# Linear attention and a gated feed-forward layer on one core: rows, maxima and exps as separate pieces, first v on ScalarE's queue, half a projection cast by Pool's DMA, a new order

## The chip, the core and the metric

The kernel runs on one core of a Trainium2 chip. Its engines work from queues of their own: TensorE (PE; PEld is its weight load), VectorE (DVE), ScalarE (ACT), GpSimd (POOL) and SyncE (SP, which here only issues DMAs). The metric is the device time of one execution in microseconds; less is better.

## The reference, cut to what matters

```python
def _attn_ref(q, k, v, w_phi):            # q, k, v: 8 batches, 8 heads, 576 rows, 64 columns
    def phi(x):
        proj = np.einsum('bhsd,df->bhsf', x, w_phi)                   # 64 -> 128
        proj = proj - np.max(np.abs(proj), axis=-1, keepdims=True)
        return np.concatenate([np.exp(proj), np.exp(-proj)], axis=-1) # 256 features
    q_p, k_p = (phi(q), phi(k))
    kv = np.einsum('bhsf,bhsd->bhfd', k_p, v)
    z = np.sum(k_p, axis=2)
    num = np.einsum('bhsf,bhfd->bhsd', q_p, kv)
    den = np.einsum('bhsf,bhf->bhs', q_p, z)[..., None] + 1e-06
    return num / den

def _moe_ref(x, w_gate, w_val, w_out):    # x: 4608 rows of 512 (the heads side by side)
    gate = np.maximum(x @ w_gate, 0.0)    # 512 -> 1536
    val = x @ w_val
    return gate * val @ w_out             # 1536 -> 512
```

The kernel returns `_moe_ref` of the attention's output, in fp32.

## The kernel before, in words

**Tiles.** Of each batch's 576 rows, 512 are handled as four chunks of 128 (`C = 4`), and the last 64, the tail, are put together with another batch's. A key item is one pair of heads of one batch, four per batch (`NU = 4`). For it TensorE transposes the keys (L235; DVE copies the result to `tT`, L238), multiplies 64-row halves with `w2` (bf16, `w_phi` twice one below the other) into two PSUM banks (rows, L260); DVE takes the maximum of the absolute value of each row (`mk`, L242); ACT takes exp of the rows with both signs (`kp`, L280) and of the maxima with both signs (`ek`, L284); POOL multiplies v with `ek` (`vs`, L246, and a column of `ek` itself, L252); TensorE multiplies `kp` with `vs` to kv and z (L309), adds the tail's share (L317; for that POOL makes `ekm`, L294, and `vsm`, L246), and DVE (batch 0) or ACT copies the 128x260 result (`kv`, L325). From batch 2 on, keys and queries are transposed by DMA.

A query piece projects columns (L343) and rows (L260), ACT takes exps (`qp`, L354 and L356), DVE maxima (`mq`), ACT a scale from them (`cq`, L362). Numerators and denominators (L379) are combined on DVE (L388, L391, reciprocal L394) and scaled on POOL (`xu`, L396), and `xu` is transposed to `xT` (L406 on TensorE for batches 0 and 1, by DMA later). The feed-forward layer takes `xT` with the value and gate weights (L434), for batch 0 in steps of 16 matmuls of 128 columns, later of four of 512; ACT copies the value half to `val_sb` (L443), DVE makes `h` from both (L447); `h` times `w_out` (L460) is copied and stored.

**The order.** `Plan.add` collects pieces of work: a function that issues a few instructions, with the engine times that a planner assumed, what a piece needs and gives, and the PSUM banks it takes. `ORDER` is a list, found by a search beforehand, of piece numbers with their banks: `43:76` issues piece 43 with banks 7 and 6, and `z22:0` issues fillers, 22 units of 128 columns of zeros times zeros into bank 0 (L930), which compute nothing that is used. All instructions of all engines are issued in this one order, and each engine runs its own in that order. So an instruction that waits holds all later ones on its engine. The fillers of `ORDER` come to 176 units, all ahead of piece 397, the first feed-forward step.

**Loads.** Before the planned part, SP's queue gets the first pairs of batch 0 in fp32, `k0 k1 v0 k2 v1 k3`, the tail of the keys (`kt`), `v2 v3` and the tail of v (`vt`). ACT's queue gets `w_phi` twice (`wf`, L939), and ACT casts each half into `w2` (L963). POOL makes the identities (L956), then copies one element of the second key pair (`gate`, L958), so that POOL and the loads behind it wait for that pair. Loads that cast fp32 to bf16 go through POOL's queue and stand in POOL's instruction stream: queries and keys (`qn`, `kn`), the three thirds each of the value, gate and output weights (`wv_sb`, `wg_sb`, L210; `wo_sb`, L217), the tails of later batches (L176) and mixed queries (L167). `LOADS` names them as pieces 0 to 42, and `ORDER` places them:

```python
LOADS = """q0 wv0 wg0 kt1 k1 wv1 wg1 vt1 v1 wv2 wg2 q1 wo0 wo1 wo2 qm0 k2 kt2 vt2 v2 q2 k3 v3 q3 qm1
...
```

In the built program the DMAs of POOL's queue take eight semaphores in turn, and those of SP's and ACT's queues eight others; a DMA that takes a semaphore is issued once the DMA that had it before has landed.

**The key item as one piece.** In `k_group` rows, maxima, exps and `ek` were one piece (`krows`), in three forms: maxima and exps of the two halves crosswise (`wide=False`, the first two items), exps first (`"late"`, the third), and maximum first (`wide=True`). `q_group` did the same for queries.

Of the kernel before, what the change touches and what calls it, by code (L numbers as in the profile page):

```python
# [19 lines left out]
class Plan:  # L20
# [8 lines left out]
    def add(  # L29
        self, rank, kind, fn, ops, needs=(), gives=None, take=(), drop=(), after=(), banks=(), hold=None, free=None  # L30
    ):
        self.pieces.append(
            (rank, kind, fn, ops, needs, gives, take, drop, after, banks, hold, free)
        )
# [12 lines left out]
ORDER = """0 z22:0 43:76 47:5 44:6 z4:4 51:0 48:1 55:3 z4:4 59:0 52:6 z26:5 60:4 3 4 1 7 5 45 8 56:2 9 49 61  # L47
z38:1 62:0 z4:1 81:1 72:6 z18:7 82:4 z5:7 63:06 84:2 67 50:3 57 46:4 53 88:5 85:6 2 68:24 11 58:0
54:1 6 83 89:4 64:01 65:6 z27:7 69:71 10 96:2 18 90 92:3 z25:0 66:6 73:40 70:7 16 z3:2 397:6 381:3
74:04 389:2 97:6 13 382:3 71:4 93:0 17 86 91:5 130 75:23 391:4 76:6 94 133 98 399:7 390:3 100:2  # L50
109:6 78:50 383:1 101:36 398:2 392:5 95:0 79:1 132 102:63 15 400:2 99:5 87:0 77:1 80:3 384:4 12 14
118 103:76 104:5 106:01 395:2 393:6 385:7 107:2 126 386:3 110:46 403:0 396:1 401:2 145 19 111:63
146:0 387:5 394:2 402:3 20 137 105:4 119 127:6 408:2 21 115:34 112:01 128 409 411:5 410 120:36 138:0
147 131 412 413 113:2 116:6 167 139 141 388:7 24 22 405:3 108:4 406 142:0 143 134:6 404:2 177 414:4
135 149 117:5 407 23 415 114:5 140:2 121:01 419:5 122:67 416 123:5 26 150:20 417:7 129 423:4 169
418:6 435:5 151:02 178:6 424:4 136:5 436:2 148:3 433:0 124:1 425:4 173 144:2 181 170:6 158 182:0 203
426:5 420:4 168 434:3 437:2 152:56 179 153:7 431:4 29 429:3 430:6 154 183 438:7 155:01 194 217 427:2
159:35 432:7 125 421:2 28 25 156:1 439:0 160:63 171 174:1 422:5 185 184:0 428:3 440:4 175 164:76
444:5 157 161:34 162:1 441:2 27 180:0 442 176:0 165:1 172:6 445 166 163 186:30 447:7 443 446 187:03
211 215 212:5 448 33 450:2 216 451 188:34 189:0 449 230 452 35 191:16 469:7 213 453:0 195:24 226  # L60
192:1 30 454:6 214 473:7 461:0 196:41 231:6 474:3 470:0 462:1 463:2 190 200:54 457:3 32 201:0 467:1
222 193 227:6 223:2 464:4 302 468:5 218 252 253 234 31 458:0 232 455:1 465:4 262 204 197:76 228
475:5 198:0 466:2 229:3 243 235:60 456:4 459:5 205:20 199 460:4 471:7 254 224 288 202 236:50 219:2
472:4 477:7 476:0 220 206:15 233:6 478 36 263:4 270 480:0 225:6 34 481 221:3 479 207:21 483:4 237:35
238:1 240:67 264 482 505:2 486:5 258 259:0 255:2 484 487 260 300 489:7 241:6 488 485 497:6 490:0
208:1 507:2 266 256 289 209:3 506:7 244:04 508:6 499:7 495:2 239 245:03 38 267:5 496:7 500:2 493:3
242 498:4 246:70 503:1 247:2 261:4 249:03 301 307 257:1 250:7 504:6 501:5 290:31 509:0 319 494:7
491:5 271:13 315 268 308:6 492:0 502:5 510:3 511:4 512:2 248 269:5 251 279 265:3 272:06 39 316:4
513:2 296 519:3 520 516:6 40 273:70 521 303 37 276:14 328 514 274:5 515 275 297:3 304:0 529:7 311
277:5 522:2 517 278 518 539:5 523 41 525:3 524 280:06 526:4 305 317 545:5 337 540:3 309 281:60 312:4  # L70
527:2 530:3 338 298 546:0 285:16 210 339 313 533:7 547:3 286:0 282:64 283:5 318:1 364 291:27 534:0
343 310:1 351 531:6 284 528:1 532:7 535:0 320:53 344:1 306:7 347 548:0 537:3 541:4 538:0 536:5 42
287 543:6 542:7 292:43 544:2 314:1 293:0 552:3 561:1 573:2 553 321:06 352:4 549:2 345 550 294:6
555:7 322:01 554 551 355 323:1 565:6 325:05 556 558:6 559 560 557 329:42 562:6 299 295 577:7 566:0
330:13 348:5 373 583:7 574:0 567:3 326:4 578:1 331:20 575:4 584:1 568:0 332:7 576:6 563:5 324 334:74
333 564:3 569:2 349 581:1 356:64 340:2 571:0 579:1 582:4 591:5 335:6 570:7 336 346:4 594:6 357:20
572:7 341 585:4 580:0 592 588:7 353 589 354:3 374 350:2 342:1 327 586 593 361:03 601:2 587 358:15
595 359:0 603:2 362:3 590 611:4 597:5 596 365:02 598:7 602:4 612:5 366:62 607:4 608:5 360 599:0
370:12 619:3 600:0 371:2 620:7 363 613:1 615:0 375:24 604:1 609:0 614:7 367:65 617:4 368:7 618:3
376:52 624:4 605:1 369 610:0 606:7 616:6 621:5 627:7 372 622 623 625 630:6 626 631 377:53 628 655:4  # L80
645:0 378:5 639:1 632 629 633:0 634:1 646:2 640:0 637:1 651:7 652:0 647:6 379:7 638:5 656:4 643:3
641:2 642:1 648:0 649:7 635:6 636:5 644:7 650:6 657:0 663:7 380 666:1 653:2 667 677:3 654:2 658
669:6 659 668 660:2 664 661 671:3 662 665 681:6 670:5 682:7 672:6 689:0 673:7 678:1 679:0 674:2
675:1 676:0 680:7 685:6 691:5 687:7 686:6 692:0 690:7 688:1 683:0 684:2 693:1 696:0 694 695 702:7
703:6 704:5 699:7 697 700 698 701"""
# [6 lines left out]
def kernel(  # L92
# [172 lines left out]
    def k_group(st, n=4, at=0, wide=True):  # L265

        banks = rows_group([(par, st["T"]) for par in range(2)], n)
        if "kp" not in st:
            st["kp"] = st["pool"].tile([P, 2, 2, 4, F], BF16, name="kp")
        kp = st["kp"][:, :, :, at : at + n]  # L270
        ek = st["ek"] = sb_s.tile([P, 8, 2], FP32, name="ek", bufs=8)[:, 0 : 2 * n]
        mk = sb_s.tile([P, 8], FP32, name="mk")[:, 0 : 2 * n]
        m = mk.rearrange("p (j i) -> p i j", i=2)
        for par in range(1 if wide else 2):
            mine = slice(0, 2) if wide else slice(par, par + 1)
            other = slice(0, 2) if wide else slice(1 - par, 2 - par)
            if wide != "late":
                row_max(m[:, mine], banks[:, mine])
            for s, sign in ((0, 1.0), (1, -1.0)):
                nc.scalar.activation(kp[:, s, other], banks[:, other], AF.Exp, scale=sign)  # L280
            if wide == "late":
                row_max(m, banks)
        for s, sign in ((0, -1.0), (1, 1.0)):
            nc.scalar.activation(ek[:, :, s], mk, AF.Exp, scale=sign)  # L284
# [47 lines left out]
    def q_group(st, i, places):  # L332
# [13 lines left out]
        banks = rows_group(halves)  # L346
# [5 lines left out]
        for s, sign in ((0, 1.0), (1, -1.0)):  # L352
            if x is y:
                nc.scalar.activation(x["qp"][:, s], cols, AF.Exp, scale=sign)  # L354
            else:
                nc.scalar.activation(x["qp"][:, s, a], cols[:, 0], AF.Exp, scale=sign)  # L356
                nc.scalar.activation(y["qp"][:, s, b], cols[:, 1], AF.Exp, scale=sign)  # L357
        m = st["m"][:, 2 * lo : 2 * lo + 8]
# [66 lines left out]
    def ffn_pieces(g):  # L425
# [102 lines left out]
        for t in range(3 if g == B else 4):  # L528
            for part in range(3):
                ops = [("PE", NF * (0.0025 + DM / 2400))]  # L530
                if part == 2:
# [16 lines left out]
                    banks=[(1, None)] if part == 0 else [],  # L548
                    hold=(g, "po", t) if part == 0 else None,
                    free=((g, "po", t), 1) if part == 2 else None,  # L550
# [22 lines left out]
    def load(fn, us, gives, take=(), eng="POOL", issue=0.9):  # L573
        plan.add(
            "load", None, fn, [(eng, issue), ("DMA", us, 0, 2.6)], gives=gives, take=take
        )
# [6 lines left out]
    def k_pieces(rank, st, start, ops, needs, take, name, banks, late=(), n=4, at=0, wide=True):  # L583
        plan.add(rank, "kT", start, ops, needs, (rank, "T"), take, late, banks=banks)
        us = 0.1 + n * 0.287, 0.08 + n * 0.206
        if wide == "late":
            ops = [("PE64", 0.055 * n), ("ACT", us[1]), ("ACT", us[1], 0), ("DVE", us[0]), ("ACT", 0.21)]
            last = 3
        elif wide:
            ops = [("PE64", 0.055 * n), ("DVE", us[0]), ("ACT", us[1]), ("ACT", us[1], 1)]  # L590
            ops += [("ACT", 0.21, 1)]
            last = 3
        else:
            ops = [
                ("PE64", 0.23),
                ("DVE", 0.6, 0),
                ("ACT", 0.48, 0),
                ("ACT", 0.48, 0),
                ("DVE", 0.6, 3),
                ("ACT", 0.48, 1),  # L600
                ("ACT", 0.48, 1),
                ("ACT", 0.21, 4),
            ]
            last = 6
# [3 lines left out]
            lambda: k_group(st, n, at, wide),  # L608
            ops,
            [(rank, "T")],  # L610
            (rank, "rows", 0),
            [],
            [(tag, 0, n, key) for tag, n, key in name],
            banks=[(2, last)],
        )

    def k_item(rank, b, u):
# [4 lines left out]
        def start():  # L622
# [3 lines left out]
            kn = inputs["kn", b]  # L626
# [10 lines left out]
        else:  # L637
# [4 lines left out]
            else:  # L642
# [9 lines left out]
                [("T4", 1, rank)],  # L652
                banks,
                [("kn" if b else "vn1", 0, NU, ("k", b))],
                wide=b > 0 or (False, False, "late", True)[u],
            )
        plan.add(
            rank,
# [414 lines left out]
```

## Time and profile before

| | us |
|---|---|
| median of 5 runs | 391.26 (388.54 to 393.53) |
| the profiled execution | 391.61 |
| its span, first to last instruction | 389.8 |
| TensorE busy | 378.0 |
| ScalarE, VectorE, GpSimd busy | 239.6, 238.6, 155.2 |
| fillers (L930), 48 matmuls | 14.0 |
| feed-forward matmuls with value and gate weights (L434) | 95.3 and 94.5 |
| matmuls with w_out (L460) | 100.0 |

A line of the timeline has the start, the duration, the engine (with q: its DMA issues), the line of the code, the operation, the tile written and those read, shapes and how many of them in a row; in brackets, the idle time before and what ended it. A line of the busy times by stretches has the stretch, its length, the busy time of PE, PEld, DVE, ACT and POOL (with the number of instructions), the granted TensorE clock (1.00 is full), the busy share of the DMA engines (it can pass 1, as transfers overlap) and GB/s. A line of the DMA issues has the tiles, the queue, the number of issues, KB of each and the median time from issue to landing. In the slices, each of 40 digits stands for a fortieth of the span, 9.7 us, in tenths.

### The profile page before, as it was taken

How to read it: one execution, taken by the hardware profiler on the slowest of the kernel's cores; microseconds unless marked ns; L12 is line 12 of the kernel's file. 1: busy time of each engine (PE TensorE's matmuls, PEld its weight loads, DVE VectorE, ACT ScalarE, POOL GpSimd, SP SyncE). 2: the span in 40 equal slices, each digit the busy share in tenths (PEclk: the TensorE clock that was granted, in tenths of full speed). 3: DMA queues.
4: the chain of work that ended last, by engine and by line, in shares of the span. 5: the costliest groups of instructions: out<-in, count | busy, mean ns of one | idle time of the engine just before them, and what ended most of it. 6: DMA issues, size and time to landing. Idle time of an engine off the chain costs nothing.

```text
span 389.8 us, 8990 instructions
## 1 busy us (share of the span) xinstructions
PE 378.0 (97%) x3620; PEld 210.0 (54%) x3620; DVE 238.6 (61%) x413; ACT 239.6 (61%) x480; POOL 155.2 (40%) x176
## 2 busy tenths in 40 slices
PE   8599999999999999999999999999999999999995
PEld 4266998555564455645454645445554444444452
DVE  4568988777885788658864866487347622522230
ACT  5639868788768889578768774576455414323411
POOL 5785963795562873381506731413420100100000
PEclk9979999999999999999999999999999999999999
DMA  8999999999399999647649930230122021002003
GB/s 219 205 238 198 170 109 211 180 240 142 49 231 171 157 162 224 104 124 123 167 77 200 193 42 3 82 69 15 27 82 56 13 69 54 14 3 108 0 5 105
DMA packets 92506, 45.22 MB, mean 116 GB/s; under 512 B 58288, under 2 KB 87984, under 8 KB 92464
## 3 DMA queue, kind: packets, MB, share of 16 engines
q1 hardware_dynamic: 63984, 30.55, 35.6%
q0 software_dynamic: 27840, 13.50, 28.2%
q10 hardware_dynamic: 640, 0.59, 0.5%
q8 instruction: 28, 0.46, 0.5%
q14 instruction: 14, 0.11, 0.1%
HBM read 37.81 MB, written 9.44 MB: 121 GB/s over the span
## 4 chain that ended last, share of the span: by engine, by line
PE 92%; DMA 4%; ACT 1%; SPq 1%; DVE 1%; issue 0%; ACTq 0%
PE pall L434 49%; PE pall L460 23%; PE pall L379 5%; PE pall L260 4%; PE pall L309 4%; PE pall L343 3%; DMA kt<-in_k_dram 2%; DMA vn<-in_k_dram 1%; PE pall L930 1%; PE pall L235 1%; PE pall L317 1%; PE pall L487 1%; SPq L158 1%; ACT kp L280 0%; ACT qp L354 0%
## 5 line engine op out<-in xcount | busy, mean ns | idle before, releaser
L447 DVE SCALAR_TENSOR_TENSOR h<-pall,val_sb 128x512 bf16<-128x512 f32 x108 | 72.7, 685 | 53.1 <-PE pall L434 43.3
L443 ACT CAST val_sb<-pall 128x512 bf16<-128x512 f32 x108 | 62.4, 597 | 66.8 <-PE pall L434 63.4
L460 PE MATMUL pall<-wo_sb,h 128*128 128x512 bf16 x420 | 100.0, 379 | 0.0
L434 PE MATMUL pall<-xT,wv_sb 128*128 128x512 bf16 (+1 forms) x528 | 95.3, 321 | 0.0
L434 PE MATMUL pall<-xT,wg_sb 128*128 128x512 bf16 (+1 forms) x528 | 94.5, 321 | 0.0
L396 POOL TENSOR_TENSOR xu<-u,r 128x512 bf16<-128x512 f32 x36 | 37.4, 1042 | 142.2 <-DVE r L394 88.4
L280 ACT ACTIVATE kp<-pall 128x1024 bf16<-128x1024 f32 (+1 forms) x78 | 70.3, 958 | 23.6 <-DVE mk L242 22.5
L246 POOL TENSOR_TENSOR vs<-vn,ek 128x1024 bf16<-128x1024 f32 x32 | 61.1, 1908 | 21.5 <-ACT ek L284 19.6
L434 PEld LDWEIGHTS <-wv_sb 128*128 128x128 bf16 x576 | 46.5, 98 | 39.8
L434 PEld LDWEIGHTS <-wg_sb 128*128 128x128 bf16 x576 | 46.1, 98 | 39.7
L242 DVE TENSOR_REDUCE mq<-pall 128x8 f32<-128x1024 f32 x36 | 44.0, 1221 | 34.8 <-PE pall L260 15.9
L460 PEld LDWEIGHTS <-h 128*128 128x128 bf16 x420 | 38.5, 98 | 41.0
L388 DVE TENSOR_TENSOR t<-pall,cq 128x455 f32<-128x455 f32 (+3 forms) x80 | 33.5, 419 | 25.0 <-PE pall L379 24.6
L242 DVE TENSOR_REDUCE mk<-pall 128x8 f32<-128x1024 f32 (+1 forms) x39 | 43.7, 1135 | 6.7 <-PE pall L260 3.4
L356 ACT ACTIVATE qp<-pall 128x512 bf16<-128x512 f32 x60 | 36.5, 608 | 6.3 <-PE pall L343 6.3
L470 ACT COPY out_sb<-pall 128x512 f32<-128x512 f32 x35 | 20.5, 590 | 31.9 <-PE pall L460 31.0
L391 DVE TENSOR_TENSOR u<-pall,t 128x455 f32<-128x455 f32 (+3 forms) x80 | 34.2, 428 | 6.9 <-POOL xu L396 0.5
L357 ACT ACTIVATE qp<-pall 128x512 bf16<-128x512 f32 x60 | 36.8, 613 | 0.0
L379 PEld LDWEIGHTS <-qp 128*128 128x128 bf16 x640 | 28.1, 98 | 13.4 <-ACT qp L354 0.5
L379 PE MATMUL pall<-kv,qp 128*128 128x65 bf16 x640 | 30.6, 193 | 0.4 <-DVE kv L325 0.3
L309 PEld LDWEIGHTS <-kp 128*128 128x128 bf16 x512 | 18.9, 97 | 3.6
L309 PE MATMUL pall<-vs,kp 128*128 128x65 bf16 x512 | 20.5, 193 | 0.0
(67 smaller groups left out, 273.3 us busy)
## 6 DMA issues: line engine op xcount, KB each, us to landing
out_dram<-out_sb SPq DMA_DIRECT2D x32, 256.0 KB, 2.5
vn<-in_v_dram SPq DMA_DIRECT2D x7, 1024.0 KB, 8.2
qn<-in_q_dram POOLq DMA_DIRECT2D x8, 512.0 KB, 8.8
kn<-in_k_dram POOLq DMA_DIRECT2D x7, 512.0 KB, 8.1
wv_sb<-in_moe_w_val_dram POOLq DMA_DIRECT2D x3, 512.0 KB, 19.6
wg_sb<-in_moe_w_gate_dram POOLq DMA_DIRECT2D x3, 512.0 KB, 11.3
wo_sb<-in_moe_w_out_dram POOLq DMA_DIRECT2D x3, 512.0 KB, 9.5
vn<-in_k_dram SPq DMA_DIRECT2D x4, 256.0 KB, 3.6
```

Of the source, the lines that this page charges most:

```text
L242: nc.vector.tensor_reduce(m, banks, axis=AX.X, op=ALU.max, apply_absolute_value=True)
L246: nc.gpsimd.tensor_tensor(dst[:, :, :, 0:D], src[:, :, None, :].to_broadcast([P, *dst.shape[1:3], D]), ek[:, :, :, None].to_broadcast([P, ...
L280: nc.scalar.activation(kp[:, s, other], banks[:, other], AF.Exp, scale=sign)
L309: nc.tensor.matmul(kv_ps[:, hh, s, :], lhsT=st["kp"][:, s, c % 2, 2 * hh + c // 2], rhs=st["vs"][:, 4 * hh + c, s, :], start=(hh == s == c ...
L356: nc.scalar.activation(x["qp"][:, s, a], cols[:, 0], AF.Exp, scale=sign)
L357: nc.scalar.activation(y["qp"][:, s, b], cols[:, 1], AF.Exp, scale=sign)
L379: nc.tensor.matmul(banks[s][:, i], lhsT=x["qp"][:, s, slot, P * blk : P * (blk + 1)], rhs=kvs[b, h // 2][:, h % 2, s, :],)
L396: nc.gpsimd.tensor_tensor(x["xu"], x["u"][:, :, 0:D], r.to_broadcast([P, 8, D]), op=ALU.mult)
L434: nc.tensor.matmul(ps[:, n * i : n * (i + 1)], lhsT=w[:, dc, P * fi : P * fi + P], rhs=xT[:, dc, lo:hi], start=(dc == 0), stop=(dc == NDC ...
L443: nc.scalar.copy(st["val", step], ps)
L447: nc.vector.scalar_tensor_tensor(st["h2"][:, fis[0] : fis[-1] + 1, lo:hi], ps.rearrange("p (a b) -> p a b", b=n), 0.0, st["val", step].rea ...
L460: nc.tensor.matmul(st["po", t], lhsT=st["h2"][:, fi, P * t : P * t + P], rhs=wo_sb[:, fi, :], start=(fi == 0), stop=(fi == NFC - 1),)
```

## The change

1. **Smaller pieces.** `k_group` becomes `k_rows`, `k_max` with `k_scales`, and `k_exps`, which `ORDER` places one by one; the crosswise form stays one piece behind its rows, for the first two items alone. `q_group` becomes `q_rows`, `q_exps` and `q_max`. There are 849 pieces in place of 705.
2. **First loads.** `w_phi` goes once to `wf` on ACT's queue, and its second half goes straight to `w2` by a casting DMA of POOL's queue (in the built program, POOL's first DMA). The four pairs of batch 0's v go on ACT's queue. Of batch 0's keys the first two pairs stay on SP's queue in fp32, and the last two go by POOL's queue in bf16, into the unused room of the same tile. The `gate` copy is gone. Key and v tails follow on SP's queue.
3. **The order** is searched anew, with other assumed times for a few loads. Its fillers come to 143 units. `LOADS` is as before.

```diff
-    def k_group(st, n=4, at=0, wide=True):
...
+    def k_rows(st, n=4):
+        st["rows"] = rows_group([(par, st["T"]) for par in range(2)], n)
+
+    def k_exps(st, n, at, pars=slice(0, 2)):
...
+        for s, sign in ((0, 1.0), (1, -1.0)):
+            nc.scalar.activation(kp[:, s, pars], st["rows"][:, pars], AF.Exp, scale=sign)
+
+    def k_max(st, n, pars=slice(0, 2)):
...
+    def k_crosswise(st):
+
+        for par in range(2):
+            k_max(st, 4, slice(par, par + 1))
+            k_exps(st, 4, 0, slice(1 - par, 2 - par))
+        k_scales(st, 4)
...
+    def wide_pieces(rank, st, n, at, done=lambda: None):
+        plan.add(
+            rank,
+            "kmax",
+            lambda: (k_max(st, n), k_scales(st, n)),
...
+        plan.add(
+            rank,
+            "kexp",
+            lambda: (k_exps(st, n, at), done()),
...
-    for hh in range(2):
-        nc.scalar.dma_start(out=wf[D * hh : D * (hh + 1)], in_=w_phi)
+    nc.scalar.dma_start(out=wf[0:D], in_=w_phi)
+    nc.gpsimd.dma_start(out=w2[D:P], in_=w_phi)
...
-    for step in "k0 k1 v0 k2 v1 k3 t v2 v3".split():
-        if step == "t":
-            load_first_tail(0)
-        else:
-            heads = slice(2 * int(step[1]), 2 * int(step[1]) + 2)
-            load_kqv(0, step[0] + "n", k if step[0] == "k" else v, nc.sync, FP32, heads)
+    late_k = inputs["kn", 0][:, 4:6].bitcast(BF16).rearrange("p a c d -> p (a c d)")
+    late_k = late_k.rearrange("p (h c d) -> p h c d", h=4, c=C)
+    for u in range(NU):
+        if u < 2:
+            load_kqv(0, "kn", k, nc.sync, FP32, slice(2 * u, 2 * u + 2))
+        load_v(0, 2 * u, 2 * u + 2, nc.scalar)
+    load_first_tail(0)
     load_tail(inputs["vt", 0], 0, 1, v, nc.sync)
...
-    gate = singles.tile([P, 1], FP32)
-    nc.gpsimd.tensor_copy(gate, inputs["kn", 0][:, 2, 0, 0:1])
+    for u in range(2):
+        nc.gpsimd.dma_start(
+            out=late_k[:, 2 * u : 2 * u + 2],
+            in_=k[0, 4 + 2 * u : 6 + 2 * u, 0:SF, :].rearrange("h (p c) d -> p h c d", c=C),
+        )
...
-        nc.scalar.copy(w2[rows], wf[rows])
+    nc.scalar.copy(w2[0:D], wf[0:D])
...
-ORDER = """0 z22:0 43:76 47:5 44:6 z4:4 51:0 48:1 55:3 z4:4 59:0 52:6 z26:5 60:4 3 4 1 7 5 45 8 56:2 9 49 61
+ORDER = """z22:0 43:76 48:5 44:6 45 z6:4 49:0 z14:2 53:5 0 50 z12:4 54:2 65:7 3 59:6 4 56 1 5 z9:4 66:4 46 67
...
```

In the built order of POOL's queue the DMAs run: half of `w_phi`, the last two key pairs of batch 0, q of batch 0, k of batch 1, value thirds 1 and 2, q of batch 1, value third 3, gate third 1, four parts of the keys' tail of batches 2 and 3, gate third 2, two parts of a mixed q, gate third 3, k of batch 2, the thirds of `w_out`. Before they ran: q of batch 0, k of batch 1, value thirds 1 to 3, gate third 1, q of batch 1, gate thirds 2 and 3, k of batch 2, `w_out` third 1, four parts of the tail. TensorE's lines move from L235, L260, L309, L343, L379, L406, L434 and L930 to L240, L265, L323, L357, L402, L429, L457 and L999.

## The prediction, made before the result was known

> **What bounds the kernel now.** I read the page's first lines, then the busy time by stretches. It splits the span into a start-up, a dense part and a tail.
>
> ```profile
> span 389.8 us, 8990 instructions
> ...
> PEclk9979999999999999999999999999999999999999
> DMA  8999999999399999647649930230122021002003
> ```
> ```profile
> 36.14:385.05 348.91, 348.78 (x3328) 192.81 (x3325) 216.60 (x372) 217.31 (x433) 132.33 (x144) 1.00 0.60 106
> 0.00:36.14 36.14, 29.26 (x294) 17.18 (x295) 22.01 (x42) 21.66 (x47) 22.87 (x33) 0.91 1.15 216
> 385.05:389.80 4.75, 0.00 (x1) 0.00 (x0) 0.00 (x0) 0.59 (x1) 0.00 (x0) 0.99 0.41 110
> ```
>
> From 36.14 on, where the first feed-forward step starts behind the last filler, TensorE idles 0.13 us in 348.91; the tail is output. So only the first 36 us have anything to give: there the DMA share is over 1 while TensorE runs fillers (L930, 14.0 us) or waits. Its longest wait is in the timeline, together with a clock that fell (0.50 from 18 to 24 us, 0.77 in 24 to 25, in one-microsecond stretches).
>
> ```profile
> 15.41 0.38 PE L930 MATMUL pall<-zeros 128*128 128x512 bf16 x1
> 19.22 0.66 PE L235 MATMUL pall<-ident,kt 128*128 128x128 f32 x2 [3.43 <-DMA kt<-in_k_dram]
> 19.67 1.06 PE L235 MATMUL pall<-ident,qn 128*128 128x128 bf16 x8
> 20.52 2.13 PE L930 MATMUL pall<-zeros 128*128 128x512 bf16 x5
> ```
>
> Then the DMA issues one by one (narrow windows; the last number is the time to landing).
>
> ```profile
> wv_sb<-in_moe_w_val_dram POOLq DMA_DIRECT2D x1, 512.0 KB, 20.1
> ...
> vn<-in_v_dram SPq DMA_DIRECT2D x1, 1024.0 KB, 18.4
> ...
> wg_sb<-in_moe_w_gate_dram POOLq DMA_DIRECT2D x1, 512.0 KB, 11.3
> ...
> qn<-in_q_dram POOLq DMA_DIRECT2D x1, 512.0 KB, 14.3
> ```
>
> Issued at 10.71, 12.52, 22.55 and 23.36, they land at 30.8, 30.9, 33.8 and 37.6: everything asked for early is in by 30.9, and the rest follows in order of issue. Last, POOL, which issues loads and scales v in one stream:
>
> ```profile
> 22.55 0.80 POOL L210 DMA_DIRECT2D wg_sb<-in_moe_w_gate_dram  x1
> 23.36 0.89 POOL L158 DMA_DIRECT2D qn<-in_q_dram  x1
> 24.23 0.77 POOL L210 DMA_DIRECT2D wg_sb<-in_moe_w_gate_dram  x1
> 25.17 0.21 POOL L294 TENSOR_TENSOR ekm<-ek,half 128x16 f32<-128x16 f32 x1 [0.17 <-ACT ek L284]
> 25.46 1.91 POOL L246 TENSOR_TENSOR vsm<-vt,ekm 128x1024 bf16<-128x1024 f32 x1
> ...
> 37.34 0.26 POOL L252 CAST vs<-ek 128x16 bf16<-128x16 f32 x1
> ```
>
> No load makes POOL wait here, and batch 1's first scaled v is ready at 37.6, before TensorE multiplies it at 41.45.
>
> **The change, part by part.** *Splitting and reordering* adds no arithmetic: the maxima, exps and matmuls are the same. *The last two head pairs of batch 0's keys* (items 2 and 3) arrive in bf16, so eight fp32 transposes (0.66 us for four, 8.52) become bf16 ones (0.22): 0.87 us of TensorE saved. Fillers fall from 176 to 143 units, inside waits: nothing.
>
> *The gate copy goes, and half of w_phi comes by Pool's DMA.* POOL no longer waits 2.9 us for the second key pair before its first load. The w_phi issue (about 0.9) pushes the identities from 1.66 to some 2.5, under the wait for the first key pair at 3.5; key pairs 2 and 3 are issued by 4.4, then batch 0's q, batch 1's k and two value thirds as now. Price: loads and v share the engines with the second key pair, which I put at 5.4 instead of 1.26+3.2=4.5; hidden behind the next item.
>
> *First v on ScalarE's queue.* Its third v pair waits for the first key pair (0.73+2.8=3.5) and its fourth for the first half of the k tail, and the copy of w_phi's first half stands behind both in ACT's order. Bounds for that copy: 4.1 (as now, 3.79 to 4.09) and 9.1 (now the tail lands at 4.09+4.7=8.8). The tail now stands directly behind the second key pair but shares engines with v and k: I take 7.6. First rows then come 2 us later than 5.57. From there ACT and POOL run by rows: exps 1.06 a pair of halves or 1.94 wide, maxima 0.68 or 1.22, v scaling 2.17 (1.91+0.26) each. Chain: rows end at 8.0, exps 9.1, second maximum 9.8, second exps 10.1, ek (0.31) 10.4, where the first scaling starts (now 8.73); ACT goes on with item 1's exps and ek to 12.8, item 2's wide exps, then the tail's ek to 15.05. POOL: 10.4+2.17; from 12.8 to 15.0; ekm to 15.3; tail to 17.45; third to 19.6; two issues (0.9+0.8) to 21.3; fourth to 23.5 (now 22.7). The second k tail, late today at 19.1, is asked for no later and transposed at 21.6, so the 3.43 us wait goes. The first numerators run at about 24.6 instead of 30.61. So far, 6 us early.
>
> *Pool's queue* is where this is given back. In the built order each software DMA takes one of eight semaphores in turn and may be issued once the earlier one on it has landed. SP shows such a wait for its own queue: the second half of v, issued at 5.71, had waited for a v issued at 1.75, landing after 3.9. Before, POOL's first eight are loads up to the second gate third, so nothing waits. Now half of w_phi and two key loads come first and a four-part k tail is pulled ahead, and POOL's stream becomes: gate third 2 behind value third 2; first x scaling; q tail behind batch 1's q (q1) and value third 3; second x scaling; gate third 3 behind gate third 1; batch 2's keys; w_out third 1; ekm; the tail's v; batch 1's first v.
>
> When do those land? The set in by 30.9 stays, key pairs 2 and 3 shrinking from 0.52 MB at 296 GB/s (the rate in 2 to 8 us) to 0.26 MB at about 200, saving 0.45. Then 30.9 to 37.64 carried gate third 1, q1 and a 0.26 MB v tail at 192 GB/s; that tail (1.35) now comes later. So q1, value third 3 and gate third 1 are all in by 30.9+6.74-1.35-0.45=35.8; in reverse, 0.5 MB each at 200 GB/s is 2.6: value third 3 at 33.2, q1 at 30.6, value third 2 at 28.0. POOL has ended the v scaling and five issues (0.8+2.5) by 26.8, so loads hold it, and a start-up up to 1.2 us worse costs nothing. After 35.8: 0.80+0.95+0.76 (issues), 0.22 (ekm), 2.17+2.17: batch 1's first v at 42.9.
>
> TensorE has the q1 transposes at 30.6. Then, in its order, 20 transposes (1.11), two column and row groups (1.08), two key row groups (0.66), five feed-forward steps of 0.89 and one x transposition (0.22): 7.5 us, so it stands at batch 1's first kv product at 38.2, or up to 40.8 with half the clock for part of it, and waits until 42.9. This wait replaces the k tail's. Behind it in order are numerators and all further feed-forward steps.
>
> What is it against now? With 55.6 ns for 128 columns, 30.6 for 65, 28 for a row matmul and 215 for 512, I summed both orders. At that product the new kernel has 335.3 us left; the old one reaches 335.3 left at 43.55, inside the feed-forward step begun at 42.76. Gain: 0.65. POOL's next scalings (2.17 each) stay ahead of TensorE (45.1 against 45 and more), so I add no second hold.
>
> *Clock.* A 3.43 us wait cost 5.2 us at half clock afterwards, 2.6 us; a 0.85 us wait (before 14.95) cost none. The new wait is 2.1 to 4.7 us, the shorter if TensorE comes in slowly, the likelier after the idle time before q1. Bounds 0 and 2.6; in proportion between the two rows, 2.1 us gives 1.3, and I take 1.4. [...]
>
> Sum: 389.8-0.65+1.4=390.55 of span. The profiled execution took 391.61, 1.81 around its span, and lies 0.35 above the median 391.26: 390.55+1.81-0.35=392.0.
>
> [...]
>
> **Rivals.** *Loads do not hold POOL*: the transfers land 3 us or more earlier, TensorE arrives and goes on at 38.2 to 40.8. For it: first numerators are 6 us early. Against: DMA is full from 2 us. Gain 43.55-38.2=5.35, less at half clock: 391.26-5.35=385.9 to 388.5, centre 386.9.
> *Transfers get slower with three queues*: 35.8 becomes later. For it: the rate is 296 with one queue of large packets and 198 (14 to 22 us) with mixed ones. At 195 instead of the mean 216 of the start-up, 33.8 us become 37.4: a hold until 46.5, and the full clock price: 391.26+2.95+2.6=396.8. It decides from a landing of gate third 1 at about 37.5.
> *The change starts no earlier and the new order is as dense*: the early part shows on no wait that ends last; only the 0.87 us count: 390.4.
>
> **How the numbers follow.** Forecast 0.45 (own range 390 to 394), first rival 0.24, second 0.20, third 0.11. Within 1% (387.35 to 395.17) is what a measurement of this kernel cannot tell from no change. The first rival is beyond that bound in most of its range, 0.17, and the forecast with a shorter hold rarely, 0.03: faster 0.20. Slower: the second rival 0.18, and holes in the new dense part 0.04, of which before shows only 0.13 us: 0.22. Same 0.58. The range leaves out the ends of both rivals: 386.3 to 396.8.
>
> **What would show it.** Right: no TensorE wait for kt at 19; first numerators (L402) near 25; POOL's second gate load issued near 28 and its third near 36, waiting for landings; a TensorE wait of 2 us or more before the first kv of batch 1 near 42; PEclk below 1 behind it. Wrong: gate third 1 landing before 32, POOL not waiting at issues, TensorE dense from 31 or 36, or holes after 50 us.

## The result, and the profile after

The changed kernel takes 390.17 us (median of 43 runs, 389.43 to 392.5) against 392.22 for the kernel before beside it (80 runs); the ratio is 0.9971, 95% interval 0.9956 to 0.9986. So it is 0.3% faster. A ratio here is of executions in the faster of two states alone, run beside each other, so it is not the quotient of the two medians. The forecast, 392.0 on a base of 391.26, had it 0.2% slower. The profiled execution took 390.36, with 388.6 of span; the forecast's span was 390.55.

The page of the changed kernel, and its busy time by stretches cut at batch 1's first kv product (42.09):

```profile
span 388.6 us, 8993 instructions
...
PEclk9998999999999999999999999999999999999998
```
```profile
0.00:42.09 42.09, 35.24 (x412) 23.50 (x413) 28.16 (x52) 27.14 (x60) 32.71 (x46) 0.96 1.22 209
42.09:384.00 341.91, 341.06 (x3200) 186.75 (x3199) 211.76 (x362) 212.39 (x419) 124.36 (x133) 1.00 0.57 104
```

The second stretch is nearly as dense as before: TensorE idles 0.85 us in 341.91. Before, the work that the forecast counted as equal took 341.50 from 43.55 on. So the gain arises ahead of 42.09: 43.55-42.09 is 1.46; 0.41 of it is lost afterwards (0.72 more idle, 0.31 less busy), and the tail is 0.15 shorter (4.60 against 4.75). 1.46-0.41+0.15 is 1.20, the difference of the spans.

TensorE's timeline ahead of that point (start, duration, engine, line, operation; in brackets the idle time before and what ended it):

```profile
8.19 0.61 PE L265 MATMUL pall<-w,tT 64*128 64x128 bf16 x8 [0.93 <-ACT w L1036]
...
24.73 0.44 PE L240 MATMUL pall<-ident,kt 128*128 128x128 f32 x2
...
27.10 0.59 PE L402 MATMUL pall<-kv,qp 128*128 128x65 bf16 x14 [0.27 <-DVE kv L339]
...
42.09 0.64 PE L323 MATMUL pall<-vs,kp 128*128 128x65 bf16 x16 [0.23 <-POOL vs L257]
```

The first rows wait for the late copy of `w_phi` (5.57 before). The second key tail is transposed at 24.73 without a wait (19.22 after 3.43 us of waiting before). The first numerators are 3.5 us early (30.61 before). At batch 1's first kv product TensorE waits for GpSimd, but for 0.23 us only. GpSimd's own timeline shows what it did meanwhile:

```profile
27.88 0.79 POOL L215 DMA_DIRECT2D wg_sb<-in_moe_w_gate_dram  x1
...
32.60 0.68 POOL L172 DMA_DIRECT2D qm<-in_q_dram  x1 [0.69 <-DMA wv_sb<-in_moe_w_val_dram]
...
35.15 0.82 POOL L215 DMA_DIRECT2D wg_sb<-in_moe_w_gate_dram  x1 [0.35 <-DMA kt<-in_k_dram]
...
39.94 1.90 POOL L251 TENSOR_TENSOR vs<-vn,ek 128x1024 bf16<-128x1024 f32 x1
41.78 0.25 POOL L257 CAST vs<-ek 128x16 bf16<-128x16 f32 x1
```

Load issues, two of which wait for landings (0.69 and 0.35 us), stand ahead of the scaling, which ends at 42.03. The row at 35.15 names a part of the key tail; by the order of the semaphores this issue waits for gate third 1, which landed at 34.86. Last, the clock and VectorE, by stretches:

```profile
20.00:30.00 10.00, 7.34 (x134) 5.82 (x132) 9.49 (x18) 5.93 (x12) 8.58 (x12) 1.00 1.25 248
30.00:36.00 6.00, 5.96 (x72) 4.37 (x72) 5.05 (x12) 5.17 (x11) 4.31 (x6) 0.72 1.40 197
```

In 20 to 30 us VectorE is busy 9.49 of 10 us while TensorE has 2.66 us idle; then the clock is at half for 3.4 us (0.72 on the mean of six).

### The profile page after: what moved, and what is told of

Read it like the earlier page. It is cut to its first block, busy times and chain, and to the rows that moved or that the text cites. A ratio compares the mean times of both kernels' runs of the same rounds, so it can differ in the third digit from the quotient of the medians.

```text
span 388.6 us, 8993 instructions
## 1 busy us (share of the span) xinstructions
PE 376.3 (97%) x3611; PEld 210.3 (54%) x3611; DVE 239.9 (62%) x413; ACT 240.1 (62%) x479; POOL 157.1 (40%) x178
## 4 chain that ended last, share of the span: by engine, by line
PE 87%; POOL 6%; issue 3%; DMA 2%; DVE 0%; ACT 0%; ACTq 0%; POOLq 0%; DVEq 0%
PE pall L457 48%; PE pall L483 23%; PE pall L402 5%; PE pall L265 4%; PE pall L323 4%; DMA kt<-in_k_dram 2%; POOL vs L251 2%; PE pall L357 2%; PE pall L331 1%; POOL vsm L251 1%; PE pall L510 1%; POOL qn L163 0%; POOL wv_sb L215 0%; POOL wg_sb L215 0%; PE pall L429 0%
## 5 line engine op out<-in xcount | busy, mean ns | idle before, releaser
L470 DVE SCALAR_TENSOR_TENSOR h<-pall,val_sb 128x512 bf16<-128x512 f32 x108 | 73.8, 687 | 74.9 <-PE pall L457 67.2
L466 ACT CAST val_sb<-pall 128x512 bf16<-128x512 f32 x108 | 63.6, 597 | 58.6 <-PE pall L457 47.5
L457 PE MATMUL pall<-xT,wv_sb 128*128 128x512 bf16 (+1 forms) x528 | 95.1, 321 | 0.5 <-ACT val_sb L466 0.5
L457 PE MATMUL pall<-xT,wg_sb 128*128 128x512 bf16 (+1 forms) x528 | 94.0, 321 | 0.0
L457 PEld LDWEIGHTS <-wv_sb 128*128 128x128 bf16 x576 | 47.0, 98 | 41.7 <-issue 0.6
L457 PEld LDWEIGHTS <-wg_sb 128*128 128x128 bf16 x576 | 46.7, 98 | 40.1
L247 DVE TENSOR_REDUCE mq<-pall 128x8 f32<-128x1024 f32 x36 | 43.8, 1220 | 17.2 <-PE pall L265 13.6
L414 DVE TENSOR_TENSOR u<-pall,t 128x455 f32<-128x455 f32 (+3 forms) x80 | 34.2, 428 | 6.5
L402 PEld LDWEIGHTS <-qp 128*128 128x128 bf16 x640 | 27.3, 98 | 11.6 <-issue 1.2
L402 PE MATMUL pall<-kv,qp 128*128 128x65 bf16 x640 | 29.7, 194 | 1.2 <-DVE u L414 0.9
L323 PE MATMUL pall<-vs,kp 128*128 128x65 bf16 x512 | 20.7, 193 | 0.2 <-POOL vs L257 0.2
L323 PEld LDWEIGHTS <-kp 128*128 128x128 bf16 x512 | 18.8, 97 | 3.6 <-issue 0.4
## 6 DMA issues: line engine op xcount, KB each, us to landing
wv_sb<-in_moe_w_val_dram POOLq DMA_DIRECT2D x3, 512.0 KB, 13.6
wg_sb<-in_moe_w_gate_dram POOLq DMA_DIRECT2D x3, 512.0 KB, 10.3
```

What stands on the lines that cost most here:

```text
L247: nc.vector.tensor_reduce(m, banks, axis=AX.X, op=ALU.max, apply_absolute_value=True)
L323: nc.tensor.matmul(kv_ps[:, hh, s, :], lhsT=st["kp"][:, s, c % 2, 2 * hh + c // 2], rhs=st["vs"][:, 4 * hh + c, s, :], start=(hh == s == c ...
L402: nc.tensor.matmul(banks[s][:, i], lhsT=x["qp"][:, s, slot, P * blk : P * (blk + 1)], rhs=kvs[b, h // 2][:, h % 2, s, :],)
L457: nc.tensor.matmul(ps[:, n * i : n * (i + 1)], lhsT=w[:, dc, P * fi : P * fi + P], rhs=xT[:, dc, lo:hi], start=(dc == 0), stop=(dc == NDC ...
L466: nc.scalar.copy(st["val", step], ps)
L470: nc.vector.scalar_tensor_tensor(st["h2"][:, fis[0] : fis[-1] + 1, lo:hi], ps.rearrange("p (a b) -> p a b", b=n), 0.0, st["val", step].rea ...
```

## The experiments

Theory 1: GpSimd's stream, issues that wait for landings ahead of batch 1's scalings, sets when TensorE goes on. Theory 2: TensorE's own start-up (the late copy, VectorE's backlog, the half clock) makes it arrive no earlier. In the changed kernel both end within 0.23 us of each other, so the trace alone can't tell. Every ratio below is to the kernel before, run beside it; one that is not far from another is read with its interval.

### v back on SyncE's queue (e1): the start-up alone

```diff
         if u < 2:
             load_kqv(0, "kn", k, nc.sync, FP32, slice(2 * u, 2 * u + 2))
-        load_v(0, 2 * u, 2 * u + 2, nc.scalar)
+            load_v(0, 2 * u, 2 * u + 2, nc.scalar)
     load_first_tail(0)
+    for u in range(2, NU):
+        load_v(0, 2 * u, 2 * u + 2, nc.sync)
```

> The changed kernel with the third and fourth pairs of batch 0's v put back on SyncE's queue behind the key tail, so that ScalarE's copy of w_phi waits for w_phi alone. The copy should then come at about 4 us instead of 7.84, and the first rows at 6 to 7 instead of 8.19. Theory 1 (GpSimd's stream of load issues and scalings sets when batch 1's first v is ready): that stream is untouched, batch 1's first kv product stays at 42.1 within 0.3, its wait for v grows by what TensorE comes earlier (0.5 to 1.5), and the time against the changed kernel is 0 (-0.3 to +0.3 us). Theory 2 (TensorE's own start-up, with the copy at 7.8 and VectorE busy without a break from 20 to 32, sets it): the kv product comes 0.5 to 1.2 us earlier and so does the end.

Measured: 391.79, ratio 1.0002 (0.9969 to 1.0036). TensorE's timeline of this run:

```profile
5.46 0.40 PE L265 MATMUL pall<-w,tT 64*128 64x128 bf16 x8
...
23.43 0.58 PE L402 MATMUL pall<-kv,qp 128*128 128x65 bf16 x14 [0.27 <-DVE kv L339]
...
38.10 1.07 PE L457 MATMUL pall<-xT,wv_sb 128*128 128x128 bf16 x16
41.97 1.04 PE L323 MATMUL pall<-vs,kp 128*128 128x65 bf16 x16 [2.81 <-POOL vs L257]
```

Everything up to there is 2.7 us or more earlier (first rows 5.46, numerators 23.43), and the kv product comes at 41.97 all the same: all is given back in a wait of 2.81 us for GpSimd. GpSimd came earlier too, and gave it back at its own issues:

```profile
29.99 0.74 POOL L172 DMA_DIRECT2D qm<-in_q_dram  x1 [2.46 <-DMA qn<-in_q_dram]
32.49 0.68 POOL L172 DMA_DIRECT2D qm<-in_q_dram  x1 [1.75 <-DMA wv_sb<-in_moe_w_val_dram]
```

Theory 1 is shown for an early start. Theory 1 missed one thing, that it would be no slower than the changed kernel: behind this wait the clock falls,

```profile
42.00:45.00 3.00, 3.00 (x44) 3.00 (x44) 1.17 (x2) 1.74 (x5) 3.00 (x3) 0.50 1.32 196
```

and the span is 389.9 against 388.6. (The clock had also been at half from 24.7 to 31.5 us; the wait covers that fall.) This is the very case that the forecast had described: an early TensorE, a hold of 2.1 us or more and a clock that pays for it.

### Issues later (e2), both edits (e12), the changed kernel again (c1)

```diff
-... 121:0 525:2 6 83:7 ... 541:2 122 16 526:7 13 115:3 527:5 101 106 152
+... 121:0 525:2 83:7 ... 541:2 122 526:7 115:3 527:5 101 106 6 16 13 152
```

Pieces 6, 16 and 13 are the issues of gate third 2, batch 2's keys and a third of `w_out`; 106 is the scaling of batch 1's first v.

> The changed kernel with three of GpSimd's load issues (gate third 2, the keys of batch 2, a third of the output weight) moved behind the scaling of batch 1's first v in the order. Without their waits for landings batch 1's first v should be ready at 39 to 40 instead of 42.03. Theory 1 (that stream alone holds TensorE): the kv product comes 1.5 to 2.5 us earlier and the end 1 to 2 us. Theory 2 (TensorE arrives at 41.85 anyhow): the wait of 0.23 goes and no more; the time is 0 to -0.3 us against the changed kernel, and later work that needs gate third 2 (near 48 us) may wait.

> Both edits of the two runs before together. If GpSimd's stream and TensorE's start-up end together by chance (0.23 us apart, as the changed kernel's trace has it), each edit alone gives under 0.3 us and both together 0.7 to 1.5 us. Theory 1 alone: the same as the issues-later run, 1 to 2 us. Theory 2 alone: the same as the run with v on SyncE's queue.

> The changed kernel itself, unedited, on the same chip as the three runs beside it: 0.9971 of before (0.994 to 1.000), and a second profile that shows how far the start-up's moments move from one execution to another (a few tenths of a microsecond by the waits for landings).

Measured: issues later 389.53, 0.9946 (0.9909 to 0.9982); both edits 389.65, 0.9945 (0.9909 to 0.998); the changed kernel again 390.23, 0.996 (0.9935 to 0.9985). The kv products of the three, each from its own timeline:

```profile
42.23 0.65 PE L323 MATMUL pall<-vs,kp 128*128 128x65 bf16 x16
```
```profile
40.30 0.65 PE L323 MATMUL pall<-vs,kp 128*128 128x65 bf16 x16
```
```profile
42.77 0.65 PE L323 MATMUL pall<-vs,kp 128*128 128x65 bf16 x16 [1.22 <-POOL vs L257]
```

With the issues moved the first v is ready at 39.3, and TensorE, arriving at 42.2, no longer waits: theory 2 holds for this kernel as much as theory 1. In the profiled executions only both edits together bring the product forward, by 1.8 us, which fits the reading that two chains end together. The times do not show it: issues later alone took 389.53, both edits 389.65, and the profiled execution of issues later (390.51) was a long one for its kernel. All intervals overlap with the changed kernel's. The second execution of the changed kernel, the longest of its 12 (392.28), shows the hold at 1.22 us and a span of 390.5: the hold moves by about 1 us between executions.

### Fillers in the waits (e10, e6, r3, e9)

```diff
-... 58:2 79 109:3 110 10 74:52 98:6 75:2 111 99 81:52 15 z15:3
+... 58:2 79 z8:1 109:3 110 10 z4:1 74:52 z14:1 98:6 75:2 111 99 z16:1 81:52 15 z15:3
```

On the changed kernel alone (e10), and on top of both edits (e6, and r3 the same once more):

> The changed kernel with the 42 filler units alone, v on ScalarE's queue and the three issues where they were. TensorE's clock should stay full after 30 us (0.72 in 30 to 36 without them) and TensorE come 0.8 to 1.3 us earlier to batch 1's first kv product. Theory 1: it then waits that much longer there for GpSimd (0.23 us before), the product stays at 42.0 within 0.4, and the time within 0.4 us of the changed kernel. Theory 2 (the clock was the bound): product and end come 0.8 to 1.3 us earlier.

> The run with both edits (v on SyncE's queue, three issues later) and 42 filler units more, placed ahead of the four waits for VectorE and ScalarE between 24 and 29 us, so that TensorE's clock does not fall after them (0.79 in 30 to 36 there). If the clock is what is left, the kv product comes 0.7 to 1.3 us before the 40.30 of that run, as long as the first v (38.7 there) is not late, and the end 0.5 to 1.2 us earlier; if the fillers only push the row projections back, or VectorE's backlog decides, 0 to 0.4 us slower.

> The run with both edits and fillers once more, unchanged: 0.987 to 0.993 of before if its first result (0.9895 from 6 runs) holds, near 0.995 if it was as the run with both edits alone (0.9945).

Measured: fillers alone 390.12, 0.9955 (0.9928 to 0.9983); both edits and fillers 388.98, 0.9895 (0.9864 to 0.9926, 6 runs), and again 389.72, 0.9922 (0.9899 to 0.9945, 12 runs). With fillers alone, the clock and the kv product:

```profile
30.00:36.00 6.00, 5.35 (x88) 4.05 (x84) 5.25 (x12) 5.79 (x12) 5.03 (x6) 1.00 1.41 198
```
```profile
41.36 0.65 PE L323 MATMUL pall<-vs,kp 128*128 128x65 bf16 x16 [0.33 <-POOL vs L257]
```

The clock stays full (0.72 without them), and the product is 0.7 us earlier, between the two theories: GpSimd's stream itself waits for an x scaling that TensorE feeds, so it moves up a little, and still holds TensorE for 0.33 us. The time can't be told from the changed kernel's (medians 390.12 and, again, 390.23). In the profiled executions product and span (387.9 against 388.6) are both 0.7 us earlier. So of the half clock there, which costs TensorE 1.7 us of work by estimate (half of 3.4 us), at most some 0.7 had reached the end: GpSimd's hold covered the rest. On top of both edits, with the same fillers:

```profile
29.94 0.62 PE L240 MATMUL pall<-ident,qn 128*128 128x128 bf16 x8 [1.54 <-DMA qn<-in_q_dram]
...
38.81 0.65 PE L323 MATMUL pall<-vs,kp 128*128 128x65 bf16 x16 [0.23 <-POOL vs L257]
...
43.28 0.64 PE L323 MATMUL pall<-vs,kp 128*128 128x65 bf16 x16 [1.43 <-POOL vs L257]
```

The product is at 38.81, 3.3 us before the changed kernel's and 1.5 before that of both edits; the ratios of these two lean the same way, but their intervals overlap. Of the 3.3 us the span keeps 1.7 (386.9). In the second profiled execution the product is at 38.21 and the span 388.3: TensorE waits 1.43 us for the second v and, at 65 us, 1.54 for keys of a later batch. This version beats both kernels: its second interval ends at 0.9945, where the changed kernel's begins at 0.9956. Its next wait, 1.43 us for the second v behind the issues just moved, was tried too, with the second scaling (112) ahead of pieces 16 and 13:

```diff
-... 101 106 6 16 13 152 123 ... 168 112 124
+... 101 106 6 112 16 13 152 123 ... 168 124
```

> The run with both edits and fillers, and besides the scaling of batch 1's second v put ahead of two of the three issues moved (the keys of batch 2 and a third of the output weight). TensorE waited 1.43 us for that second v there (kv product at 43.28). Theory 1 (GpSimd's order of issues and scalings decides each v): the second v is ready 1.7 us earlier, the wait falls under 0.3 and the end is 0.8 to 1.5 us earlier than in that run; if the later landings of keys and output weight, or the third v behind them, give it back, within 0.4 us of it.

Measured: 389.92, 0.9942 (0.9914 to 0.997). The wait for the second v is gone (its product at 44.20 without one), but in the profiled execution q of batch 1 landed late, TensorE waited 2.34 us for it at 29 us, and all that followed was later. No gain over the filled version is shown; which landing is late differs between executions. Issues later with fillers, but with v left on ScalarE's queue, was not run, so whether the early start is needed stays open.

### Which part of the change carries it (e4, e5, e8, r1, r2, e7)

The first loads with the old order (e4: to the kernel before, part 2 of the change and nothing else), and the new order with the old first loads (e5: to the changed kernel, the same lines turned round). Of both, the lines that say it shortest, e4 as it stands and e5 with the signs exchanged:

```diff
-        nc.scalar.dma_start(out=wf[D * hh : D * (hh + 1)], in_=w_phi)
+    nc.gpsimd.dma_start(out=w2[D:P], in_=w_phi)
...
-    for step in "k0 k1 v0 k2 v1 k3 t v2 v3".split():
+        load_v(0, 2 * u, 2 * u + 2, nc.scalar)
...
-    nc.gpsimd.tensor_copy(gate, inputs["kn", 0][:, 2, 0, 0:1])
+        nc.gpsimd.dma_start(
+            out=late_k[:, 2 * u : 2 * u + 2],
...
-            kn = inputs["kn", b]
+            kn, u0 = (inputs["kn", b], u) if b or u < 2 else (late_k, u - 2)
```

> The kernel before, its order and pieces untouched, with the change's first loads only: w_phi's second half cast by GpSimd's DMA, v of batch 0 on ScalarE's queue, the late two key pairs as bf16 by GpSimd's DMA, and no gate copy. If the first loads alone carry the gain (the wait of 3.43 us for the key tail at 19.2 goes), the time is 1 to 3 us below before. If the annealed order is needed to turn it into time (theory 1: GpSimd's later stream, which the old order keeps, decides), it is within 0.5 us of before; the late copy of w_phi (7.8 instead of 5.4) can make it up to 1.5 us slower.

> The changed kernel's pieces and order with the first loads of the kernel before (w_phi twice in fp32, all keys and v of batch 0 in fp32 on SyncE's queue, the gate copy on GpSimd). The loads-only run gave 0.9965 of before with the old order, against 0.9971 for the whole change. If the loads carry the whole gain and the order none, this is 1.000 (0.998 to 1.002) of before; if each carries it alone, because the new order too takes the key tail's transposes out of the wait (24.7 instead of 19.2 us), it is 0.996 to 0.998; theory 1 adds that GpSimd's issues, which the order keeps, hold batch 1's first kv product to 41.5 or later whatever the start is.

Measured: loads only 390.47, 0.9965 (0.9932 to 0.9997); order only 393.57, 1.0013 (0.9981 to 1.0044). The loads alone give as much as the whole change. In their run the key tail's wait is short, and the clock is full from 20 to 36 us:

```profile
19.42 0.41 PE L235 MATMUL pall<-ident,kt 128*128 128x128 f32 x2 [1.59 <-DMA kt<-in_k_dram]
```

The order alone is held where theory 1 says; its GpSimd, and its TensorE:

```profile
33.52 0.74 POOL L172 DMA_DIRECT2D qm<-in_q_dram  x1 [2.70 <-DMA qn<-in_q_dram]
36.03 0.68 POOL L172 DMA_DIRECT2D qm<-in_q_dram  x1 [1.77 <-DMA wv_sb<-in_moe_w_val_dram]
...
38.57 0.82 POOL L215 DMA_DIRECT2D wg_sb<-in_moe_w_gate_dram  x1 [0.80 <-DMA kt<-in_k_dram]
```
```profile
45.51 0.65 PE L323 MATMUL pall<-vs,kp 128*128 128x65 bf16 x16 [3.58 <-POOL vs L257]
```

The same order-only kernel with the three issues moved (the edit of e2):

> The order-only kernel (new order and pieces, old first loads; 1.0013 of before) with the three load issues of GpSimd moved behind the scaling of batch 1's first v. If GpSimd's issues are what the new order loses with late landings, the wait of 3.58 us for the first v goes, the kv product comes at 41.9 to 42.6 instead of 45.51, and the time falls to 0.993 to 0.997 of before. If TensorE then waits for a later landing instead (gate third 2, batch 2's keys), it stays at 0.999 to 1.002.

Measured: 392.4, 0.9978 (0.9948 to 1.0008). The product still comes at 45.43, though with no wait there: in this execution TensorE had waited 4.63 us, from 17 us on, for the first tail's scaled v. The direction is the expected one, the intervals overlap, and whether the order would gain by itself stays open.

Three single edits of the kernel before: v on ScalarE's queue (e8), the late keys by GpSimd's casting DMA and no gate copy (r1), only no gate copy (r2):

```diff
-            load_kqv(0, step[0] + "n", k if step[0] == "k" else v, nc.sync, FP32, heads)
+            load_kqv(0, step[0] + "n", k if step[0] == "k" else v, nc.sync if step[0] == "k" else nc.scalar, FP32, heads)
```
```diff
-    for step in "k0 k1 v0 k2 v1 k3 t v2 v3".split():
+    for step in "k0 k1 v0 v1 t v2 v3".split():
...
-    nc.gpsimd.tensor_copy(gate, inputs["kn", 0][:, 2, 0, 0:1])
+        nc.gpsimd.dma_start(
+            out=late_k[:, 2 * u : 2 * u + 2],
...
```
```diff
-    nc.gpsimd.tensor_copy(gate, inputs["kn", 0][:, 2, 0, 0:1])
```

> The kernel before with one edit: the four v pairs of batch 0 on ScalarE's queue; keys in fp32 and w_phi twice as before. It tells whether the second queue alone brings the key tail earlier. If it does, the wait of 3.43 us at 19.2 shrinks to 1.6 or less and the time goes to 0.996 to 0.998 of before; if the bf16 keys by GpSimd's DMA do it (fewer packets on SyncE's queue), the wait stays above 2.5 us and the time is within 0.5 us of before, or up to 1 us above it, since the copies of w_phi now stand behind v's issues.

> The kernel before with the last two key pairs of batch 0 as bf16 by GpSimd's casting DMA and without the gate copy, which would hold them; w_phi twice and v on SyncE's queue as before. If the late keys carry the gain of the loads (0.87 us of fp32 transposes gone, two transfers fewer on SyncE's queue before the key tail), the time is 0.995 to 0.998 of before, and the wait for the second key tail (3.43 us) is under 2. If they need v on ScalarE's queue beside them, it is 0.999 to 1.001.

> The kernel before without the gate copy on GpSimd, nothing else. GpSimd's loads go out up to 2.9 us earlier. If that alone makes later landings earlier, the time is 0.995 to 0.998; if the first keys and v lose what those loads gain, since the DMA engines are full from 2 us, 0.999 to 1.004.

Measured: v on ScalarE's queue 392.98, 1.0001 (0.9975 to 1.0027); late keys 390.88, 0.9966 (0.9938 to 0.9994); no gate copy 397.18, 1.011 (1.0079 to 1.0142). The first rows with v on ScalarE's queue, and the second key tail with the late keys, each from its own timeline:

```profile
9.10 0.90 PE L260 MATMUL pall<-w,tT 64*128 64x128 bf16 x8 [3.65 <-ACT w L963]
```
```profile
20.75 0.41 PE L235 MATMUL pall<-ident,kt 128*128 128x128 f32 x2 [0.89 <-DMA kt<-in_k_dram]
```

The late keys alone give as much as the whole change: the wait for the key tail is 0.89 us instead of 3.43, and the mean clock is 1.00 from 0 to 20 us and in each later stretch up to 50 us. Whether the shorter transposes or the two transfers fewer ahead of the tail do it was not separated. The second queue brings nothing that was measured (1.0001) and makes the copy of `w_phi` late (first rows 9.10 instead of 5.57). Without the gate copy, and with nothing put ahead of them, GpSimd's big loads start at 1.60 instead of 4.65 us and share the engines with what is needed first: the third key pair lands at about 10.3 instead of 6.5, the fourth at 13.5 instead of 8.5, and over the first 20 us the engines move 195 GB/s instead of 212. In the change two small key loads stand ahead of them, and the big loads start at 4.29; that this does what the gate copy did is inferred, not tested.

Last, the loads-only kernel with v on SyncE's queue (the edit of e1; e7), and that kernel with 36 filler units more in its wait for the key tail (e11):

```diff
-... 62:0 z4:1 81:1
+... 62:0 z40:1 81:1
```

> The loads-only kernel with the third and fourth pairs of batch 0's v on SyncE's queue behind the key tail. The copy of w_phi then comes at about 4 us and TensorE's wait of 1.7 us for it goes. If that wait is paid in time, 0.5 to 1.5 us less than the loads-only run (0.9965 of before); if the fillers and the wait for the second key tail (1.6 us at 17.8) take it up, since that tail is no earlier or even later behind v on the same queue, the same within 0.4 us.

> The loads-only kernel with v on SyncE's queue (0.9972 of before), and in its wait of 2.27 us for the second key tail 36 filler units more, so that TensorE is busy there though the tail lands no earlier. It measures the price of the clock by itself: in that run the clock fell to 0.84 in 20 to 30. If the fall of the clock is what that wait costs beyond itself, 1.0 to 1.8 us faster than that run, the clock 1.00 in 20 to 30; if not, the same within 0.4 us.

Measured: 391.32, 0.9972 (0.9944 to 1.0), and 391.25, 0.9975 (0.9951 to 0.9999): neither gains over loads only. In the first, the start is earlier by about a microsecond, but TensorE gets the key tail at 19.53 us, against 19.42 in the loads-only run, so the wait grows from 1.59 to 2.27 us, and the clock falls behind it:

```profile
19.53 0.46 PE L235 MATMUL pall<-ident,kt 128*128 128x128 f32 x2 [2.27 <-DMA kt<-in_k_dram]
```
```profile
20.00:23.00 3.00, 3.00 (x17) 1.37 (x15) 1.12 (x2) 0.00 (x0) 3.00 (x3) 0.50 1.21 208
```

The second is inconclusive: in its profiled execution the key pairs came late (4.1 us of waits before 11 us) and the wait to be filled was not there.

## Why the prediction was wrong, step by step

- *Late copy of `w_phi`, first scaling, end of the key tail's wait*: right, each later than forecast by 0.6 to 1.2 us. First rows 8.19 (forecast 2 us behind 5.57), first scaling 11.19 (10.4), the fourth ended 24.7 (23.5), no wait for the tail at 19.
- *First numerators at 24.6*: 27.10. The chain of ACT and GpSimd was summed, VectorE was not; it was busy 9.49 of 10 us there, and TensorE waited 0.67, 0.27 and 0.91 us for it and 0.81 for ACT's exps.
- *Landings*: three of four right within 1 us: q1 at 29.78 (30.6), value third 3 at 32.31 (33.2), gate third 1 at 34.86 (35.8). Value third 2 came at 23.89 (28.0), 4.1 us early, so gate third 2 was issued at 27.88 without a wait: "near 28" came true by luck.
- *GpSimd's stream gives the early start back*: right, and shown by the v-on-SyncE run. Third gate issue at 35.15 ("near 36"), batch 1's first v at 42.03 (42.9).
- *TensorE's arrival at 38.2 to 40.8 and a wait of 2.1 to 4.7*: wrong, 41.85 and 0.23. The q1 transposes started at 32.43, not 30.6, behind the late numerators, and the 7.5 us of work took 9.42, partly at half clock. TensorE was dense from 31 to 38 us, which the forecast had named as a sign of being wrong. The v-on-SyncE run has the forecast's case: arrival at 39.16, wait 2.81.
- *Gain 0.65*: 1.46, of which 0.41 was lost again behind 42.09.
- *Clock, "I take 1.4"*: this is the step that failed. Forecast span minus measured is 390.55-388.6, 1.95: 1.4 from the clock, 0.81 from the gain, less 0.26 for what came later (0.41-0.15). The term was hung on the hold. The hold, 0.23 us, was too short for it, and behind it the clock was full. The clock had fallen earlier, at 30.8 us, and most of that fall was covered by the same hold (filling the waits kept the clock at 1.00 and the time at 0.9955 against 0.996). A cost before a wait that ends at a fixed time costs nothing; I had added it behind one.

The first rival (loads do not hold GpSimd) fails: the issues wait, and TensorE waits for them as soon as it comes early. The second fails as well: gate third 1 was in by 34.86, 2.6 us ahead of the point from which it decides. The third names nearly the measured time (390.4), not its way: the start is earlier, the order of itself gains nothing that was measured (1.0013), and the late keys give 0.9966 alone.

Two numbers of the rivals were wrong. The 0.87 us set a row's duration (0.66) against a sum of steps (0.22); from start to start four fp32 transposes took 0.49 us (8.52 to 9.01) and four bf16 ones 0.22 (14.10 to 14.32, changed kernel), which saves 0.54. And the second rival's hold until 46.5 does not follow from a landing at 37.4: with the same 7.1 us behind it the hold ends at 44.5, and the sum is 394.8.

## What to carry to other kernels

When two chains end within a few tenths of a microsecond of each other, shortening one may show nothing: here an early start alone was given back in a wait, with a slower clock behind it (0.50 from 42 to 45 us), and later issues alone brought nothing that can be told from the changed kernel. Both together did not either; with fillers besides, the kernel was 0.8 to 1% faster than before, and clear of the change. Sum every engine's stream up to the point in question, the one that seems idle too, and before adding a cost ask whether it lies before or behind a wait that ends at a fixed time. Loads asked for early were not free here, with a DMA share of 1.01 over the first 20 us (without the gate copy 1.1% slower): ask first for what is needed first.

## What was not expected of the hardware

In these profiles the granted clock fell in pieces of one length. Added up from one-microsecond stretches it was at half for 3.4 us in the changed kernel (30.8 to 34.2), around the end of the hold of the v-on-SyncE run (41.7 to 45.1) and behind the wait of 2.27 us (19.8 to 23.2), and for 6.8 us, twice that, before (17.6 to 24.5). Without the gate copy it comes to about 13.6 us, four times 3.4, worked out from the mean clock of 0.71 over the first 20 us and 0.67 from 20 to 23. A wait of 1.59 us left it full; 2.27 and 2.81 us did not, nor did 2.66 us of idle time scattered over ten. What sets the length, and how much idle time it takes, was not shown. The price in time is then, as an estimate, 1.7 us (half of 3.4) for each such piece, wherever TensorE has work and nothing later covers it.

A second queue for the first loads did not raise the rate by itself: in the run of v on ScalarE's queue the engines moved 214 GB/s over the first 20 us, 212 before, and the ratio was 1.0001.
